# Linear-attention block with gated MLP: denominators, their broadcast and the first gate/up tiles put into other gaps

## The chip, the cores and the metric

The kernel runs on one core of one Trainium2 chip. The metric is the device time of one execution in microseconds (us). The engines of a core are called here as the profile does: PE (TensorE, matmuls), PEld (its weight loads), DVE (VectorE), ACT (ScalarE), POOL (GpSimd) and SP (the queue that issues the transfers).

## What is computed

The input x has 2048 tokens of 640 values. It is normalized once, and the result xn feeds two branches:

```python
xn = layernorm(x)
qkv = xn @ wqkv                                # 32 heads of 20
phi = lambda t: where(t > 0, t + 1, exp(t)) + 1e-6
pq, pk = phi(q), phi(k)
kv  = einsum("bhsd,bhse->bhde", pk, v)         # one 20x20 matrix for each head
z   = pk.sum(over s)
num = einsum("bhqd,bhde->bhqe", pq, kv)
den = einsum("bhqd,bhd->bhq", pq, z) + 1e-6
s   = (num / den) @ wo
g   = silu(((xn @ w_gate) * (xn @ w_up)) @ w_down)   # inner width 1728
out = x + s * g
```

All matrices are bf16. The attention is linear: keys and values are first summed up to `kv` and `z`, and then applied to the queries.

## The kernel before

The five engines have a program each and are tied together by counting semaphores only; the order of the work on each engine is written out by hand. Tokens are cut into 16 tiles of 128 rows, four of which make a chunk of 512 columns (`NCH` = 4 chunks `c`). The model width of 640 is cut into five tiles of 128 (`KD`, indices `k`, `m`, `i`), the inner width of 1728 into 14 (`NF`, index `f`), the last of which has 64 rows. The on-chip accumulator PS has eight banks of 512 fp32 columns.

The stages follow one another like this:

1. *Set-up* (L251 to L266, L635). POOL writes constants and index tables, then sets to zero three areas: `Emat` (L264), `KVm` (L265) and `recd` (L266). DVE makes the identity matrix (L636) from an index table and sets to one the columns of `v_tm` that yield the sum z (L720).
2. *Normalization and transposes.* DVE takes the statistics of the tiles in order (L662 to L665); ACT takes those of chunk 2 (L536, L537). DVE applies them (L688); PE transposes (L315), DVE copies the result to `xnT` (L698).
3. *Queries, keys, values.* PE forms a query tile (L343) or a key or value tile (L360 for 512 columns, L361 for 128), ACT takes exponentials (L553, L560) or copies values (L563), DVE finishes phi (L707 and L709, L716 and L718). Within the second chunk DVE also makes a mask of the heads, `Emat` (row h has ones in the 20 columns of head h) and `ET` in `emit_setup2` (L638 to L656).
4. *Key-value products* (L396 to L405): five accumulations over 16 tiles. ACT takes out the column z (L588), DVE masks the product into `KVm` (L762) and forms `Zm` (L768).
5. *Denominators* (L408 to L411): for each chunk five matmuls give 32 heads x 512 tokens, on partitions 0 to 31 of banks 4 to 7. DVE adds the epsilon (L771), takes the reciprocal (L773), and converts it into the chunk's columns of `recd` (L775).
6. *Numerators* `ot` (L413 to L422): 20 tiles of 128 features x 512 tokens, two or three matmuls each, in banks 0 and 1 by turns; ACT copies them to `oT` (L593).
7. *Broadcast and projection* (L424 to L458). `emit_rbc` spreads the reciprocals of a chunk over the features with one matmul for each feature tile, `Emat` as the weights and `recd` as the moving operand (L433), in banks 4 and 5; DVE multiplies `oT` by the result (L782). `emit_s` multiplies by `Wo` (L450 for 512 columns, L451 for 128), ACT copies the result to `s_tm` (L599). The order is rbc 0, rbc 1, s 0, rbc 2, s 1, rbc 3, s 2, s 3.
8. *Gate and up, down* (L465 to L510): for each of the 4 x 14 tiles five gate matmuls (L478) and five up matmuls (L484); gate tiles use banks 0 and 1 by turns, up tiles banks 2 and 3. ACT copies gate (L608), DVE multiplies it by up into `hT` (L794). Down (L502, L503), sigmoid (L617) and the final products (L806 to L813) of a chunk follow when gate and up of the next chunk have been issued.

The transfers are issued by SP: x, `Wqkv` after the first twelve tiles of x, `Wo`; `Wu` when the last value tile is done, `Wg` and the down weights when the last key-value product is done, as they take the places of arrays no longer in use.

The waits around the change: an `ot` tile waits until ACT has copied the tile two before it (L418); an rbc matmul waits for the reciprocals of its chunk (L429) and for DVE's product two before it (L431); a projection chunk waits for all five products of its chunk (L442); the first gate tile waits for ACT's last copy of the projection (L473).

Of the kernel before, what the change touches and what calls it, by code (L numbers as in the profile page):

```python
# [6 lines left out]
ALU = mybir.AluOpType  # L7
# [5 lines left out]
def bass_recurrent_scan__linear_attn_block__glu_gated_bilinear__prompt_kernel(  # L13
# [40 lines left out]
    with es:  # L54
# [62 lines left out]
        R9a = es.enter_context(nc.sbuf_tensor("R9a", [P, S], bf16))  # L117
        R9b = es.enter_context(nc.sbuf_tensor("R9b", [P, 2 * CW], f32))
        recd = R9a[:, :]
        dtmp = R9b[0:H, 0:CW]  # L120
        rtmp = R9b[0:H, CW:2 * CW]
# [41 lines left out]
        s_pool2 = sem("s_pool2")  # L163
# [21 lines left out]
        s_rec = sem("s_rec")  # L185
        s_ot = sem("s_ot")
# [63 lines left out]

        block = es.enter_context(nc.Block())  # L251

        @block.gpsimd
        def _(eng):
            nc.gpsimd.memset(consts[:, 0:1], EPS_LN)
            nc.gpsimd.memset(consts[:, 1:2], EPS_DEN)
            nc.gpsimd.memset(consts[:, 2:4], 0.0)
            nc.gpsimd.memset(zcol[:, :], 0.0)
            nc.gpsimd.iota(tI160[:, :], pattern=[[P, KD], [-DH, H]], base=0, channel_multiplier=1)
            nc.gpsimd.iota(ti128[:, :], pattern=[[1, P]], base=0, channel_multiplier=-1).then_inc(s_pself, 1)  # L260
            eng.wait_ge(s_pself, 1)
            nc.gpsimd.tensor_copy(ti128f[:, :], ti128[:, :])
            nc.gpsimd.tensor_copy(tI160f[:, :], tI160[:, :]).then_inc(s_pool, 1)
            nc.gpsimd.memset(Emat, 0.0)  # L264
            nc.gpsimd.memset(KVm_flat, 0.0)  # L265
            nc.gpsimd.memset(recd, 0.0).then_inc(s_pool2, 1)  # L266
# [31 lines left out]
        def _(eng):  # L298
# [96 lines left out]
            eng.wait_ge(s_vact, NT)  # L395
            for i in range(KD):  # L396
                hmin, nh = headband(i)
                col0 = (DH + 1) * hmin
                N = (DH + 1) * nh
                bb = i % 2  # L400
                if i >= 2:
                    eng.wait_ge(s_kvbdve, i - 1)
                for t in range(NT):
                    ins = mm(PS[:, 512 * bb:512 * bb + N], pk_tm[:, t, P * i:P * i + P], v_tm[:, t, col0:col0 + N], start=(t == 0), stop=(t == NT - 1))  # L404
                ins.then_inc(s_kvb, 1)  # L405

            eng.wait_ge(s_kvbdve, KD)
            for c in range(NCH):  # L408
                for k in range(KD):
                    ins = mm(PS[0:H, 512 * (4 + c):512 * (4 + c) + CW], Zm[:, k, :], pqT[:, k, CW * c:CW * c + CW], start=(k == 0), stop=(k == KD - 1))  # L410
                ins.then_inc(s_den, 1)  # L411

            for c in range(NCH):  # L413
                for m in range(KD):
                    j = KD * c + m
                    ks = band(m)
                    if j >= 2:
                        eng.wait_ge(s_otact, j - 1)  # L418
                    ob = j % 2
                    for ii, k in enumerate(ks):  # L420
                        ins = mm(bank(ob), KVm[:, k, P * m:P * m + P], pqT[:, k, CW * c:CW * c + CW], start=(ii == 0), stop=(ii == len(ks) - 1))
                    ins.then_inc(s_ot, 1)  # L422

            def emit_rbc(c):  # L424
                for m in range(KD):
                    j = KD * c + m
                    if j == 0:
                        eng.wait_ge(s_erdy2, 1)
                    eng.wait_ge(s_rec, max(c + 1, 1 + (j % 2)))  # L429
                    if j >= 2:  # L430
                        eng.wait_ge(s_onorm, j - 1)  # L431
                    rb = 4 + (j % 2)
                    mm(bank(rb), Emat[:, P * m:P * m + P], recd[:, CW * c:CW * c + CW], start=True, stop=True).then_inc(s_rbc, 1)  # L433
# [4 lines left out]
            def emit_s(c):  # L438
                for tt in range(TPC):
                    t = TPC * c + tt  # L440
                    if tt == 0:
                        eng.wait_ge(s_onorm, KD * (c + 1))  # L442
                        if c == 0:
                            eng.wait_ge(dma_wo, 16)
                            eng.wait_ge(s_rec, NCH)
# [8 lines left out]
            emit_rbc(0)  # L454
            for c in range(NCH):
                if c + 1 < NCH:
                    emit_rbc(c + 1)
                emit_s(c)  # L458
# [5 lines left out]

            def emit_gu(c):  # L465
                for f in range(NF):
                    m = NF * c + f
                    rows = P if f < NF_FULL else F_REM
                    if m == 0:
                        eng.wait_ge(dma_wg, 16)  # L470
                        eng.wait_ge(dma_wu, 16)
                        eng.wait_ge(s_otact, KD * NCH)
                        eng.wait_ge(s_sact, NT)  # L473
                    if m >= 2:
                        eng.wait_ge(s_gcp, m - 1)
                    gb = m % 2
                    for k in range(KD):
                        ins = mm(PS[0:rows, 512 * gb:512 * gb + CW], Wg[:, k, P * f:P * f + rows], xnT[:, k, CW * c:CW * c + CW], start=(k == 0), stop=(k == KD - 1))  # L478
                    ins.then_inc(s_gu, 1)
                    if m >= 2:  # L480
                        eng.wait_ge(s_h, m - 1)
                    ub = 2 + m % 2
                    for k in range(KD):
                        ins = mm(PS[0:rows, 512 * ub:512 * ub + CW], Wu[:, k, P * f:P * f + rows], xnT[:, k, CW * c:CW * c + CW], start=(k == 0), stop=(k == KD - 1))  # L484
                    ins.then_inc(s_gu, 1)
# [20 lines left out]
            emit_gu(0)  # L506
# [6 lines left out]
        def _(eng):  # L513
# [57 lines left out]
            pending_sqrt = [c for c in range(2, NCH) if c not in ACT_SUM_CHUNKS]  # L571
# [13 lines left out]
            for i in range(KD):  # L585
                bb = i % 2
                eng.wait_ge(s_kvb, i + 1)
                act(zcol[:, i:i + 1], PS[:, 512 * bb + DH:512 * bb + DH + 1], ACT.Copy).then_inc(s_kvbz, 1)  # L588
            for c in range(NCH):
# [4 lines left out]
            for t in range(NT):  # L594
                if t == 0:
                    eng.wait_ge(s_tr, NTR)
                eng.wait_ge(s_s, t + 1)
                sb = 6 if (t % 2 == 0) else 2
                act(s_tm[:, t, :], slot2(sb, D), ACT.Copy).then_inc(s_sact, 1)  # L599

            def emit_g_act(c):
                for f in range(NF):
                    m = NF * c + f
                    rows = P if f < NF_FULL else F_REM
                    eng.wait_ge(s_gu, 2 * m + 1)
                    if m >= RG:
                        eng.wait_ge(s_h, m - RG + 1)
                    act(g_sb[0:rows, m % RG, :], PS[0:rows, 512 * (m % 2):512 * (m % 2) + CW], ACT.Copy).then_inc(s_gcp, 1)  # L608
# [10 lines left out]
            emit_g_act(0)  # L619
# [6 lines left out]
        def _(eng):  # L626
# [11 lines left out]
            def emit_setup2():  # L638
                eng.wait_ge(s_pool2, 1)
                eng.wait_ge(s_erdy, 1)  # L640
                v.tensor_copy(
# [78 lines left out]
            tok_ones = dmark(v.memset(R4[:, :].rearrange("p (g j) -> p g j", j=DH + 1)[:, :, DH:DH + 1], 1.0))  # L720
# [6 lines left out]
            for c in ACT_SUM_CHUNKS:  # L727
                emit_mvtiny(c)
# [3 lines left out]
            dve_stats3_done = False  # L732
            tok_mask = None
            for c in range(NCH):
                if c + 2 < NCH:
                    emit_Tcp(c + 2)
                if c == 0:
                    for cc in range(3, NCH):
                        if cc not in ACT_SUM_CHUNKS:
                            emit_stats(cc)  # L740
# [3 lines left out]
                for tt in range(TPC):  # L744
                    emit_kdve_tile(TPC * c + tt)
                    if qc is not None:
                        emit_qdve_tile(qc, tt)
                    if c == 0 and tt == 1:
                        for cc in range(3, NCH):
                            emit_apply(cc)  # L750
# [3 lines left out]

            eng.wait_ge(s_dself, tok_mask)
# [13 lines left out]
            for c in range(NCH):  # L769
                eng.wait_ge(s_den, c + 1)  # L770
                tok = dmark(v.tensor_scalar(dtmp, PS[0:H, 512 * (4 + c):512 * (4 + c) + CW], EPS_DEN, None, op0=ALU.add))  # L771
# [3 lines left out]
                v.tensor_copy(recd[0:H, CW * c:CW * c + CW], rtmp).then_inc(s_rec, 1)  # L775
                eng.wait_ge(s_rec, c + 1)
            for c in range(NCH):
# [5 lines left out]
            eng.wait_ge(s_ot, KD * NCH)  # L783

            def emit_h(c):
                hb = hT[c % 2]
                for f in range(NF):
                    m = NF * c + f
                    rows = P if f < NF_FULL else F_REM
                    if f == 0 and c >= 2:  # L790
                        eng.wait_ge(s_y, TPC * (c - 1))
                    eng.wait_ge(s_gcp, m + 1)
                    eng.wait_ge(s_gu, 2 * m + 2)
                    v.tensor_tensor(hb[0:rows, f, :], PS[0:rows, 512 * (2 + m % 2):512 * (2 + m % 2) + CW], g_sb[0:rows, m % RG, :], ALU.mult).then_inc(s_h, 1)  # L794
# [20 lines left out]
            emit_h(0)  # L815
# [32 lines left out]
```

## Time and profile before

| | us |
|---|---|
| median of 4 runs | 355.93 |
| lowest, highest | 354.06, 356.73 |
| span of the profiled execution | 354.9 |

Where the stages lie in the profiled execution, by its timeline:

| stage | from | to |
|---|---|---|
| set-up, statistics, first transposes | 0 | 22.1 |
| queries, keys, values | 22.1 | 101.5 |
| key-value products | 101.6 | 107.8 |
| denominators | 107.8 | 112.3 |
| `ot` tiles | 112.5 | 126.1 |
| broadcasts and projection | 126.1 | 163.3 |
| gate and up, down, end | 163.3 | 354.9 |

A line of the timeline has the start, the length (both us), the engine, the line in the code, the operation, output and input names, the shape, and the number of instructions that were merged; in brackets stands how long the engine had been idle before, and who released it. Busy lengths of PE are modelled and overlap, since matmuls are pipelined: the distance between the starts of two matmuls tells what one takes of PE's time, the length doesn't. R is the name of most work areas of the kernel, PS that of the accumulator, R9a that of `recd`, R9b that of the denominators' work area.

### The profile page before, as it was taken

The page shows a single profiled execution, that of the slowest core. Times are in us where ns is not written, and L with a number is a line of the kernel's source. Part 1 is how long each engine was busy: PE and PEld are TensorE (multiplying, and loading weights), DVE is VectorE, ACT ScalarE, POOL GpSimd, SP SyncE. Part 2 cuts the span into 40 slices and gives each one's busy share as a digit, 9 for nine tenths or more (in the row PEclk, how much of TensorE's full clock was granted, in tenths as well). Part 3 has the DMA queues.
Part 4 walks back from the last instruction along what each step waited for, and adds up shares of the span by engine and source line. Part 5 has one row for each costly group of instructions (what it writes and reads, how often), then busy time and mean ns, then how long its engine had stood idle before and what let it go on. Part 6 is the DMA issues. An engine that isn't in the chain of part 4 may idle for free.

```text
span 354.9 us, 4525 instructions
## 1 busy us (share of the span) xinstructions
PE 315.5 (89%) x1806; PEld 154.6 (44%) x1840; DVE 186.7 (53%) x312; ACT 116.8 (33%) x192; POOL 6.4 (2%) x15
## 2 busy tenths in 40 slices
PE   0277898999988969898999999999999999999993
PEld 0232444555573214454444444554444544445451
DVE  7876979666547992411333333365332563335555
ACT  1182373555532823333222222213221222221120
POOL 7000000000000000000000000000000000000000
PEclk9999999999999987999999999999999999999998
DMA  7930000000059600005300000011000110000111
GB/s 217 340 109 0 2 0 3 0 2 0 3 178 359 212 0 0 2 0 186 112 0 2 1 0 3 0 39 37 0 2 0 37 39 0 0 2 18 39 55 38
DMA packets 11124, 18.06 MB, mean 51 GB/s; under 512 B 672, under 2 KB 9184, under 8 KB 11104
## 3 DMA queue, kind: packets, MB, share of 16 engines
q1 hardware_dynamic: 11104, 17.78, 14.5%
q8 instruction: 14, 0.23, 0.3%
q14 instruction: 6, 0.05, 0.0%
HBM read 15.16 MB, written 2.62 MB: 50 GB/s over the span
## 4 chain that ended last, share of the span: by engine, by line
PE 77%; DVE 15%; ACT 4%; issue 2%; POOL 0%; POOLq 0%; DVEq 0%; ACTq 0%
PE PS L478 17%; PE PS L484 17%; PE PS L502 14%; PE PS L360 8%; PE PS L343 5%; PE PS L450 5%; PE PS L503 4%; DVE R9b L773 4%; PE PS L361 2%; DVE R L782 2%; PE PS L404 2%; PE PS L451 1%; DVE R L636 1%; DVE statsb L663 1%; DVE statsb L662 1%
## 5 line engine op out<-in xcount | busy, mean ns | idle before, releaser
L794 DVE TENSOR_TENSOR R<-PS,R 128x512 bf16<-128x512 f32 (+1 forms) x56 | 38.6, 690 | 90.1 <-PE PS L484 90.1
L478 PE MATMUL PS<-xnT,R 128*128 128x512 bf16 (+1 forms) x277 | 69.1, 380 | 0.9 <-ACT R L599 0.9
L484 PE MATMUL PS<-xnT,R 128*128 128x512 bf16 (+1 forms) x271 | 69.1, 379 | 0.6
L502 PE MATMUL PS<-R 128*128 128x512 bf16 (+1 forms) x216 | 62.8, 380 | 0.0
L608 ACT ACTIVATE R<-PS 128x512 bf16<-128x512 f32 (+1 forms) x56 | 33.4, 597 | 85.7 <-PE PS L478 81.0
L503 PE MATMUL PS<-R 128*128 128x128 bf16 x224 | 49.0, 219 | 0.5 <-issue 0.2
L360 PE MATMUL PS<-R,xnT 128*128 128x512 bf16 x155 | 44.2, 379 | 1.5 <-DVE R L718 1.5
L478 PEld LDWEIGHTS PS<-xnT,R 128*128 128x128 bf16 (+1 forms) x280 | 27.0, 99 | 34.9 <-ACT R L608 2.1
L484 PEld LDWEIGHTS PS<-xnT,R 128*128 128x128 bf16 (+1 forms) x280 | 27.6, 99 | 32.8
L502 PEld LDWEIGHTS PS<-R 128*128 128x128 bf16 x224 | 21.8, 97 | 31.6 <-issue 8.9
L361 PE MATMUL PS<-R,xnT 128*128 128x128 bf16 x160 | 35.0, 219 | 0.3
L806 DVE TENSOR_TENSOR R<-PS,R 128x640 f32<-128x640 f32 x16 | 13.2, 824 | 31.1 <-ACT R L617 31.1
L617 ACT ACTIVATE R<-PS 128x640 f32<-128x640 f32 x16 | 11.3, 703 | 55.2 <-PE PS L503 55.2
L343 PE MATMUL PS<-xnT,R 128*128 128x512 bf16 x96 | 27.1, 425 | 2.5 <-DVE R L709 1.5
L315 PE MATMUL PS<-R 128*128 128x128 bf16 x80 | 7.8, 265 | 19.6 <-DVE R L688 16.8
L360 PEld LDWEIGHTS PS<-R,xnT 128*128 128x128 bf16 x160 | 15.6, 98 | 20.7 <-issue 1.2
L450 PE MATMUL PS<-Wo,R 128*128 128x512 bf16 x78 | 23.7, 405 | 0.0
L503 PEld LDWEIGHTS PS<-R 128*128 128x128 bf16 x224 | 21.9, 98 | 0.0
L599 ACT ACTIVATE R<-PS 128x640 bf16<-128x640 f32 x16 | 11.3, 703 | 25.0 <-PE PS L451 25.0
L782 DVE TENSOR_TENSOR R<-PS,R 128x512 bf16<-128x512 f32 x20 | 12.8, 686 | 12.3 <-PE PS L433 12.3
L451 PE MATMUL PS<-Wo,R 128*128 128x128 bf16 x80 | 18.2, 227 | 0.1
L343 PEld LDWEIGHTS PS<-xnT,R 128*128 128x128 bf16 x100 | 9.9, 106 | 15.9 <-issue 4.4
(72 smaller groups left out, 283.3 us busy)
## 6 DMA issues: line engine op xcount, KB each, us to landing
R<-in_A_x_dram SPq DMA_DIRECT2D x16, 160.0 KB, 3.7
R<-in_A_x_dram SPq DMA_DIRECT2D x4, 640.0 KB, 7.7
out_dram<-stage SPq DMA_DIRECT2D x16, 160.0 KB, 1.8
R<-in_A_wqkv_dram SPq DMA_DIRECT2D x1, 2400.0 KB, 11.8
R<-in_B_w_up_dram SPq DMA_DIRECT2D x1, 2160.0 KB, 8.0
R<-in_B_w_gate_dram SPq DMA_DIRECT2D x1, 2160.0 KB, 9.2
R<-in_B_w_down_dram SPq DMA_DIRECT2D x1, 2080.0 KB, 14.7
Wo<-in_A_wo_dram SPq DMA_DIRECT2D x1, 800.0 KB, 11.6
```

Of the source, the lines that this page charges most:

```text
L343: ins = mm(bank(qb), Wqkv[:, k, P * m:P * m + P], xnT[:, k, CW * c:CW * c + CW], start=(k == 0), stop=(k == KD - 1))
L360: mm(PS[:, 512 * kb:512 * kb + 512], xnT[:, k, P * t:P * t + P], Wqkv[:, k, wcol:wcol + 512], start=(k == 0), stop=(k == KD - 1))
L361: ins = mm(PS[:, 512 * (kb + 1):512 * (kb + 1) + D - 512], xnT[:, k, P * t:P * t + P], Wqkv[:, k, wcol + 512:wcol + D], start=(k == 0), st ...
L450: mm(PS[:, 512 * sb:512 * sb + 512], oT[:, k, P * t:P * t + P], Wo[:, k, 0:512], start=(k == 0), stop=(k == KD - 1))
L451: ins = mm(PS[:, 512 * (sb + 1):512 * (sb + 1) + D - 512], oT[:, k, P * t:P * t + P], Wo[:, k, 512:D], start=(k == 0), stop=(k == KD - 1))
L478: ins = mm(PS[0:rows, 512 * gb:512 * gb + CW], Wg[:, k, P * f:P * f + rows], xnT[:, k, CW * c:CW * c + CW], start=(k == 0), stop=(k == KD ...
L484: ins = mm(PS[0:rows, 512 * ub:512 * ub + CW], Wu[:, k, P * f:P * f + rows], xnT[:, k, CW * c:CW * c + CW], start=(k == 0), stop=(k == KD ...
L502: mm(PS[:, 512 * yb:512 * yb + 512], hb[0:rows, f, P * tt:P * tt + P], w_d(f, rows, 0, 512), start=(f == 0), stop=(f == NF - 1))
L503: ins = mm(PS[:, 512 * (yb + 1):512 * (yb + 1) + D - 512], hb[0:rows, f, P * tt:P * tt + P], w_d(f, rows, 512, D), start=(f == 0), stop=(f ...
L608: act(g_sb[0:rows, m % RG, :], PS[0:rows, 512 * (m % 2):512 * (m % 2) + CW], ACT.Copy).then_inc(s_gcp, 1)
L782: v.tensor_tensor(oT[:, m, CW * c:CW * c + CW], bank(4 + (j % 2)), oT[:, m, CW * c:CW * c + CW], ALU.mult).then_inc(s_onorm, 1)
L794: v.tensor_tensor(hb[0:rows, f, :], PS[0:rows, 512 * (2 + m % 2):512 * (2 + m % 2) + CW], g_sb[0:rows, m % RG, :], ALU.mult).then_inc(s_h, 1)
```

## The change

It moves and reshapes the work between the key-value products and the gate/up stage, so that the engines have it in other forms and at other places:

- *POOL's three large memsets go.* `recd` is now written in full; the parts of `KVm` that are read but not written by the mask are set to zero by DVE (eight memsets of 112 to 124 columns) after its last key tile; the ones of `v_tm` are set by DVE in four parts in the third and fourth chunk.
- *Denominators on 128 partitions.* The four 128-token tiles of a chunk go to partitions 0 to 31, 32 to 63, 64 to 95 and 96 to 127 (`tile_position`): 80 matmuls of 128 columns instead of 20 of 512. DVE's three operations then have 128x128 for 32x512.
- *They are spread* in groups of eight behind the `ot` tiles 2 to 11.
- *The broadcast* needs, for each of the four groups, weights with zeros outside the group's 32 rows: `Erep4`, made by PE from `Emat` with a selection matrix `Sel4` (two matmuls for each group, behind the first four key-value products) and copied by ACT. A broadcast tile is four matmuls of 128 columns instead of one of 512.
- *Order.* The broadcasts of chunk 0 stand between the `ot` tiles of chunk 3. Behind each broadcast of the chunks 1 to 3 stand two matmuls of a gate/up tile of chunk 0; a fourth gate/up tile stands ahead of the last projection chunk. ACT and DVE take the copies and products of these four tiles in between.
- *Banks.* So that they can run beside the projection, all gate tiles of chunk 0 use bank 0, all its up tiles bank 1; from chunk 1 on it is banks 0 and 1, 2 and 3 as before. The wait for ACT's last projection copy moves to the first gate/up tile of chunk 1.

```diff
-            nc.gpsimd.memset(Emat, 0.0)
-            nc.gpsimd.memset(KVm_flat, 0.0)
-            nc.gpsimd.memset(recd, 0.0).then_inc(s_pool2, 1)
...
+            def emit_erep(g):
+                eb = [2, 4, 6, 2][g]
...
+                mm(PS[:, 512 * eb:512 * eb + 512], Sel4[0:H, g, :], Emat[0:H, 0:512], start=True, stop=True)
+                mm(PS[:, 512 * (eb + 1):512 * (eb + 1) + D - 512], Sel4[0:H, g, :], Emat[0:H, 512:D], start=True, stop=True).then_inc(s_erepmm, 1)
...
-                for k in range(KD):
-                    ins = mm(PS[0:H, 512 * (4 + c):512 * (4 + c) + CW], Zm[:, k, :], pqT[:, k, CW * c:CW * c + CW], start=(k == 0), stop=(k == KD - 1))
-                ins.then_inc(s_den, 1)
+            den_items = [(c, k, g) for c in range(NCH) for k in range(KD) for g in range(TG)]
+            def emit_den(n):
...
+                        ins = mm(PS[H * g:H * g + H, 512 * (4 + c):512 * (4 + c) + P], Zm[:, k, :], pqT[:, k, CW * c + P * g:CW * c + P * g + P], start=(k == 0), stop=(k == KD - 1), tile_position=(0, H * g))
...
                     ins.then_inc(s_ot, 1)
+                    if j >= 2:
+                        emit_den(8)
...
-                    mm(bank(rb), Emat[:, P * m:P * m + P], recd[:, CW * c:CW * c + CW], start=True, stop=True).then_inc(s_rbc, 1)
+                    for g in range(TG):
+                        ins = mm(PS[:, 512 * rb + P * g:512 * rb + P * g + P], Erep4[:, g, P * m:P * m + P], recd[:, c, :], start=True, stop=True)
+                    ins.then_inc(s_rbc, 1)
+                    if filler is not None:
+                        for _ in range(2):
+                            if filler:
+                                filler.pop(0)()
...
-            emit_rbc(0)
+            emit_ot(NCH - 1, lambda m: emit_rbc(0, None, [m]))
             for c in range(NCH):
+                filler = []
+                if c < EARLY_F:
+                    for step in range(2 * KD):
+                        filler.append((lambda cc=c, st=step: emit_gu_step(0, cc, st)))
                 if c + 1 < NCH:
-                    emit_rbc(c + 1)
+                    emit_rbc(c + 1, filler)
+                while filler:
+                    filler.pop(0)()
                 emit_s(c)
...
+                toks = dmark(v.memset(Sel4[0:H, :, :], 0.0))
+                eng.wait_ge(s_dself, toks)
+                for g in range(TG):
+                    dmark(v.tensor_copy(Sel4[0:H, g, H * g:H * g + H], ident128[0:H, 0:H]))
...
-            tok_ones = dmark(v.memset(R4[:, :].rearrange("p (g j) -> p g j", j=DH + 1)[:, :, DH:DH + 1], 1.0))
+                    if (c == NCH - 2 and tt == 0) or (c == NCH - 1 and tt >= 1):
...
+                        dmark(v.memset(R4[:, :].rearrange("p (g j) -> p g j", j=DH + 1)[:, nh4 * cc:nh4 * cc + nh4, DH:DH + 1], 1.0))
...
+                if b0 > lo:
+                    dmark(v.memset(KVm[:, i, lo:b0], 0.0))
+                if hi > b1:
+                    tok_mask = dmark(v.memset(KVm[:, i, b1:hi], 0.0))
```

## The prediction, made before the result was known

> **What bounds the kernel now.** I read the page first, then the chain of waits, the timeline from 0 to 34 us and from 106 to 170 us, and last the busy times by stretch. The page says that TensorE is the engine to follow:
>
> ```profile
> PE 315.5 (89%) x1806; PEld 154.6 (44%) x1840; DVE 186.7 (53%) x312; ACT 116.8 (33%) x192; POOL 6.4 (2%) x15
> PE   0277898999988969898999999999999999999993
> PEclk9999999999999987999999999999999999999998
> ```
>
> From the 19th slice on (163 us, gate, up and down) PE is full: 175.6 of 176.7 us. Nothing is to be won there unless matmuls are moved out of it. The loss lies before: in the first three slices, and in the 15th and 16th (124 to 142 us), where PE thins out and the clock drops. The stretches between the end of the key-value products and gate/up (columns: stretch, its length, then busy us and instructions of PE, weight load, DVE, ACT, POOL, then the clock):
>
> ```profile
> 112.23:126.11 13.88, 13.04 (x51) 3.62 (x53) 13.57 (x10) 10.91 (x19) 0.00 (x0) 1.00 0.62 225
> 126.11:133.03 6.92, 4.24 (x12) 1.00 (x10) 6.51 (x11) 0.80 (x2) 0.00 (x0) 0.81 0.00 0
> 133.03:140.47 7.44, 7.39 (x40) 3.78 (x40) 0.93 (x2) 2.11 (x3) 0.00 (x0) 0.72 0.00 0
> 140.47:143.50 3.03, 1.87 (x8) 0.67 (x8) 2.56 (x5) 0.70 (x1) 0.00 (x0) 1.00 0.00 0
> ```
>
> From 126.11 PE waits for DVE, and the first block of the output projection (133.03 on) runs at a reduced clock. The timeline shows what DVE did:
>
> ```profile
> 123.43 3.34 DVE L773 RECIPROCAL R9b<-R9b 32x512 f32<-32x512 f32 x1
> 126.81 0.41 DVE L775 CAST R9a<-R9b 32x512 bf16<-32x512 f32 x1
> 128.09 0.38 PE L433 MATMUL PS<-R9a,R 128*128 128x512 bf16 x1 [1.38 <-DVE R L782]
> 128.69 0.38 PE L433 MATMUL PS<-R9a,R 128*128 128x512 bf16 x1 [0.22 <-DVE R L782]
> ```
>
> Four reciprocals of 3.34 us run on 32 of 128 lanes; the scaling of `oT` (L782, 0.69 us) starts only after the last, and then sets a pace of about 0.63 us for broadcast matmuls that need 0.216 us. At the start, DVE and not the loads is late:
>
> ```profile
> 2.06 5.07 DVE L636 TENSOR_SCALAR R<-ti128f 128x128 bf16<-128x128 f32 x1 [2.06 <-POOL tI160f L263]
> 4.19 2.94 DVE L662 BATCH_NORM_STATS2 statsb<-R 128x6 f32<-128x320 bf16 x1
> 5.24 1.80 POOL L266 MEMSET R9a<- 128x2048 bf16 x1
> 7.21 0.21 DVE L665 BATCH_NORM_AGGREGATE mv<-statsb 128x2 f32<-128x12 f32 x1
> ```
>
> L636 takes 5.07 us, though a similar operation (L645, 128x160) takes 0.22. It ends at 7.13, just behind POOL's last memset (7.04), and the statistics started at 4.19 end with it.
>
> **What the Trainium skill says.** "SBUF — State Buffer", section "SBUF: two separate sides": VectorE and GpSimd share a port pair, held for a whole instruction, and the loser is blocked. The 5.07 us agree. "TensorEngine Tiling (Array Packing)", section "Key Properties": a change of the tiling mode drains TensorE. The trace has one such change without another wait:
>
> ```profile
> 110.85 1.46 PE L410 MATMUL PS<-R 128*32 128x512 bf16 x6
> 112.23 0.76 PEld L421 LDWEIGHTS PS<-R 128*128 128x128 bf16 x5 [0.42 <-issue]
> 112.46 1.46 PE L421 MATMUL PS<-R 128*128 128x512 bf16 x5 [0.16 <-issue]
> ```
>
> The twenty L410 start 0.216 us apart from 107.81, so the last starts at 111.92 and the next should at 112.14; it starts at 112.46. The change cost 0.32 us. "TensorE: Matmul & The Clock Gate", section "What's actually happening": the clock halves after a mostly idle window of about 3.4 us. It agrees: between 133.03 and 137.2 a pair of projection matmuls (512 and 128 columns) takes 0.53 us, later 0.27.
>
> **The change part by part.**
>
> *Start.* The POOL memsets go. L636 then takes about 0.22 us and the first tile's statistics run from 4.19: 0.36 + 0.40 + the hand-over give an aggregate at 5.05 for 7.21. That is -2.1 us (-1.5 to -2.9). The later tiles, 3.7 us after issues 0.45 us apart, are there in time; the next limit, the landing of `Wqkv` at 6.4 + 11.8 = 18.2, stays ahead of the first query matmul (22.12, then 20.0).
>
> *Memsets on DVE.* The key mask stage gets a memset of 32x512 (0.48 us by L720's row) and four 32x32 copies (about 0.1 each): 0.9 us. DVE has no gap from 53.75 to 64.4, and PE's L360 at 62.28 starts right after L718 (61.40 + 0.82), so all of it is on the path: +0.9 (0.7 to 1.1). The ones for `v_tm` (four memsets of 128) lie in gaps of DVE before L716 (0.3 to 1.4 us). The zeros of `KVm`, 944 elements in eight memsets, 0.9 us plus their starts, fit in DVE's 1.62 us of idle before L762. Both at nothing.
>
> *Erep4.* Four pairs of 512 and 128 columns, 4 x 0.27 = 1.1 us, between the key-value products (no other wait there), with two mode changes each, since Sel4 has 32 rows. Exits cost 0.32; entries aren't shown, between 0 and 0.32. I take 0.25 for any change: entries a bit cheaper. 8 x 0.25 = 2.0. Sum +3.1 (1.1 to 3.7). The four ACT copies (0.70 each, by L599) fit beside the 1.07 us of the next product.
>
> *Denominators among the `ot` tiles, 107.81 to 129.56 (end of the first broadcast chunk), 21.75 us now.* The 20 matmuls of 512 columns become 80 of 128 into four column groups: 80 x 0.056 = 4.5 us. They are put as groups of 8 behind ten `ot` tiles: 20 mode changes, 20 x 0.25 = 5.0 us. New sum: two tiles without (5 matmuls, 1.1), ten tiles (26 x 0.216 = 5.6) + 4.5 + 5.0, three tiles at ACT's pace (3 x 0.65 = 1.95), the last chunk with its five broadcasts (13 x 0.216 + 20 x 0.056 = 3.9): 22.1 us, +0.3. ACT's 0.65 a tile no longer counts, as a tile takes PE 1.5 us. DVE's chain shrinks to a quarter in columns: 3.34/4 for the reciprocal, about 1.4 us in all for 4.5; the fourth is over while the next three tiles run, so no wait remains.
>
> *First projection block, 129.56 to 140.47, 10.9 us.* Broadcast of the second chunk 20 x 0.056 = 1.1 (the ten gate/up matmuls beside it, 2.16, are owed anyway) and 20 pairs at full clock, 5.4: 6.6, so -4.35. This needs PE kept warm.
>
> *Broadcasts of chunks 2 and 3.* 2.77 us each now (140.47 to 143.24, 148.62 to 151.39). With two gate/up matmuls behind each, one step takes PE 0.224 + 0.432 = 0.66 us, DVE's pace is 0.63: the wait is filled. 1.1 each, -3.3.
>
> *Projection to gate/up.* PE's wait for ACT's last copy (0.9 us before L478) moves to the second chunk, where it is long over: -0.9.
>
> *One bank each for gate and up in the first chunk.* Up's bank is free when DVE is done: it starts 0.27 after the last up matmul's slot, takes 0.69, PE sees it 0.06 to 0.15 later: 1.02 to 1.11 us against 1.08 of gate matmuls. ACT's (0.20 + 0.60 + 0.15) fits. +0.5 for ten tiles (0 to 1.0).
>
> Sum: -2.1 + 0.9 + 3.1 + 0.3 - 4.35 - 3.3 - 0.9 + 0.5 = -5.85; 355.93 - 5.85 = 350.1 us.
>
> **The rivals.** *Mode changes are free.* For it: weight loads are otherwise drawn ahead everywhere. Against it: the 0.32 us. Then 28 x 0.25 = 7.0 us less: 343.1. *The denominators eat the gain.* All 28 changes cost 0.32 (+2.0), and weight loads of the column groups aren't hidden, so that a small matmul takes 0.1 us (the 97 ns of a weight load in the row of L410; +3.5): 355.6. For it: each of the 80 has its own load, where now 20 loads stand beside 512 columns. Against it: loads stay hidden beside 147 columns in L404. *Slower.* In addition the thinned `ot` stage halves the clock for two windows, as at 130.4 to 137.2 (6.8 us at half clock, +3.4), and the single banks cost their 1.0: 355.6 + 3.4 + 0.5 = 359.5. Against it: PE's array would still be some 60% occupied, where the window that brought it on had four broadcasts, 0.9 us, in 3.4.
>
> **How the numbers follow.** Forecast 0.52, free changes 0.20, gain eaten 0.18, slower 0.10. The range runs from next to the free case, 343.5, to beyond the third, 356.0, and leaves the slower case out. Faster by over 1% (under 352.4) takes in the second case and most of the first, where the change cost may run somewhat higher: 0.66; within 1%: 0.24; slower: 0.10.
>
> **What would show it.** L636's successor near 0.2 us and the first query matmul near 20.0; gaps of 0.2 to 0.3 us around each group of eight denominators; no half clock after the `ot` stage; no PE wait for the broadcasts; 3.3 us from the first broadcast of chunk 2 to the next projection; gate/up tiles of the first chunk 2.16 to 2.25 us apart. A group of eight should lengthen its tile by 0.45 + 0.5 = 0.95 us: the forecast is wrong if that is over 1.2 or under 0.7, or if the reduced clock is still there.

## The result, and the profile after

The changed kernel takes 341.43 us (median of 10 executions; 341.28 to 342.53) against 355.45 us (median of 16, with the first four; 353.17 to 356.73). The ratio is 0.961, with a 95% interval of 0.958 to 0.963: 14.0 us less, where 5.8 us were forecast. The direction was right; the time lies below the range, and even below the rival with free mode changes (343.1). Executions of the changed kernel lie in two groups about 1 us apart (341.3 to 341.5, and 342.5), and the profiled ones of each differ in how soon PE reaches its full pace in the query stage; the one shown below, 341.45 us, has it early, the profiled one of before has it late.

The page of the changed kernel first:

```profile
PE 307.8 (91%) x1931; PEld 155.7 (46%) x1968; DVE 172.9 (51%) x328; ACT 119.8 (35%) x196; POOL 1.4 (0%) x12
PE   0477888999988999999999999999999999999993
PEclk9999999999999999999999999999999999999998
```

PE has no thin slice left in the middle, and the reduced clock there is gone.

The busy times by stretch, cut where the stages begin and end; columns: stretch, its length, then busy us and instructions of PE, weight load, DVE, ACT, POOL, then the clock. After:

```profile
18.86:97.95 79.09, 70.44 (x451) 36.57 (x461) 58.33 (x131) 40.11 (x62) 0.00 (x0) 1.00 0.02 7
97.95:106.33 8.38, 7.41 (x89) 5.76 (x91) 2.68 (x17) 3.67 (x9) 0.00 (x0) 1.00 0.74 264
106.33:122.50 16.17, 15.64 (x149) 6.24 (x150) 8.42 (x16) 11.37 (x20) 0.00 (x0) 1.00 0.78 275
122.50:126.25 3.75, 3.48 (x32) 2.10 (x31) 3.67 (x7) 1.17 (x2) 0.00 (x0) 1.00 0.02 4
126.25:131.69 5.44, 5.39 (x40) 3.07 (x40) 1.07 (x2) 2.11 (x3) 0.00 (x0) 1.00 0.00 0
131.69:134.97 3.28, 3.28 (x32) 2.05 (x31) 2.85 (x5) 1.30 (x2) 0.00 (x0) 1.00 0.00 0
156.70:339.60 182.90, 176.01 (x950) 83.52 (x968) 75.31 (x100) 44.25 (x70) 0.00 (x0) 0.99 0.09 29
```

Before, the stretches that answer to them are:

```profile
22.12:101.58 79.46, 72.30 (x451) 37.07 (x461) 57.04 (x119) 40.11 (x62) 0.00 (x0) 1.00 0.00 1
101.58:107.81 6.23, 5.49 (x80) 5.30 (x80) 2.25 (x10) 0.85 (x5) 0.00 (x0) 1.00 0.95 344
107.81:129.56 21.75, 19.03 (x75) 5.87 (x77) 20.05 (x16) 11.71 (x20) 0.00 (x0) 1.00 0.59 207
171.95:354.90 182.95, 176.26 (x950) 83.70 (x967) 75.98 (x101) 43.55 (x69) 0.00 (x0) 0.99 0.04 15
```

The last row of each block starts with the fifth gate tile, up to which both kernels have done the same work. From there they take the same time; the whole difference, 171.95 - 156.70 = 15.25 us in these two executions, lies ahead of it. That is a little more than the medians show, because the two differ in PE's pace in the query stage. The changed kernel has a second profiled execution (342.48 us, `after_again` below) with the late pace, in which the fifth gate tile starts at 157.73: with the same pace on both sides the difference is 171.95 - 157.73 = 14.2 us.

One more thing has to be known for the table. In the profiled execution of the changed kernel the first `ot` matmul has no record: its weight load is there at 106.10, and the matmul started at about 106.11, not at the 106.33 at which the stretches above are cut (how this is seen is told below). The table uses 106.11.

By stage, with 2.16 us of gate/up work taken out of each stretch that holds a moved tile:

| stage | forecast | measured in the traces |
|---|---|---|
| start to first query matmul | -2.1 | 18.86 - 22.12 = -3.3 |
| queries, keys, values (memsets on DVE) | +0.9 | 79.09 - 79.46 = -0.4; with the same pace 80.17 - 79.46 = +0.7 |
| key-value products, Erep4 | +3.1 | 8.16 - 6.23 = +1.9 |
| `ot`, denominators, first broadcasts | +0.3 | 16.39 - 21.75 = -5.4 |
| second broadcasts, first projection (129.56 to 140.47 before) | -4.35 | 3.75 + 5.44 - 2.16 - 10.91 = -3.9 |
| broadcasts of chunks 2 and 3 | -3.3 | 2 x (3.28 - 2.16 - 2.77) = -3.3 |
| projection to gate/up | -0.9 | the rest, -1.0 |
| single banks in chunk 0 | +0.5 | 182.90 - 182.95 = 0.0 |

So one row is far off: the stage with the denominators, by 5.7 us. Its timeline (PE alone) shows two groups of eight:

```profile
108.22 0.29 PE L439 MATMUL PS<-R 128*32 128x128 bf16 x8
108.45 0.82 PE L453 MATMUL PS<-R 128*128 128x512 bf16 x3
109.20 0.29 PE L439 MATMUL PS<-R 128*32 128x128 bf16 x8
109.43 0.39 PE L453 MATMUL PS<-R 128*128 128x512 bf16 x1
```

Three `ot` matmuls from 108.45 need 3 x 0.216 = 0.65 us, so the slot of the last ends at 109.10. The group starts at 109.20, and the next `ot` matmul at 109.43. A group of eight lengthens its tile by 0.33 us; the forecast had 0.95.

### The profile page after: what moved, and what is told of

Its sections match the earlier page's. It is cut to its first block, busy times and chain, and to the rows that moved or that the text cites. A ratio compares the mean times of both kernels' runs of the same rounds, so it can differ in the third digit from the quotient of the medians.

```text
span 339.6 us, 4796 instructions
## 1 busy us (share of the span) xinstructions
PE 307.8 (91%) x1931; PEld 155.7 (46%) x1968; DVE 172.9 (51%) x328; ACT 119.8 (35%) x196; POOL 1.4 (0%) x12
## 4 chain that ended last, share of the span: by engine, by line
PE 82%; DVE 10%; ACT 4%; issue 2%; DMA 1%; ACTq 0%; DVEq 0%
PE PS L525 18%; PE PS L531 18%; PE PS L577 15%; PE PS L373 7%; PE PS L496 5%; PE PS L356 5%; PE PS L578 4%; PE PS L453 4%; PE PS L374 2%; PE PS L427 2%; DVE statsb L754 1%; PE PS L497 1%; DVE statsb L753 1%; PE PS L473 1%; DVE R L809 1%
## 5 line engine op out<-in xcount | busy, mean ns | idle before, releaser
L531 PEld LDWEIGHTS PS<-xnT,R 128*128 128x128 bf16 (+1 forms) x280 | 27.1, 99 | 31.3 <-DVE R L886 2.1
L525 PEld LDWEIGHTS PS<-xnT,R 128*128 128x128 bf16 (+1 forms) x280 | 26.7, 99 | 32.0 <-ACT R L679 1.7
L705 ACT ACTIVATE R<-PS 128x640 f32<-128x640 f32 x16 | 11.3, 703 | 55.2 <-PE PS L578 55.2
L356 PE MATMUL PS<-xnT,R 128*128 128x512 bf16 x96 | 25.2, 402 | 3.2 <-DVE R L800 2.3
L496 PE MATMUL PS<-Wo,R 128*128 128x512 bf16 x78 | 21.8, 379 | 0.0
L497 PE MATMUL PS<-Wo,R 128*128 128x128 bf16 x80 | 17.5, 219 | 0.1
L635 ACT ACTIVATE R<-PS 128x640 f32<-128x640 f32 x16 | 11.3, 705 | 16.4 <-PE PS L374 16.3
```

What stands on the lines that cost most here:

```text
L356: ins = mm(bank(qb), Wqkv[:, k, P * m:P * m + P], xnT[:, k, CW * c:CW * c + CW], start=(k == 0), stop=(k == KD - 1))
L496: mm(PS[:, 512 * sb:512 * sb + 512], oT[:, k, P * t:P * t + P], Wo[:, k, 0:512], start=(k == 0), stop=(k == KD - 1))
L497: ins = mm(PS[:, 512 * (sb + 1):512 * (sb + 1) + D - 512], oT[:, k, P * t:P * t + P], Wo[:, k, 512:D], start=(k == 0), stop=(k == KD - 1))
```

## The experiments

All start from the changed kernel (341.43 us).

**The POOL memsets put back.**

```diff
             nc.gpsimd.tensor_copy(tI160f[:, :], tI160[:, :]).then_inc(s_pool, 1)
+            nc.gpsimd.memset(Emat, 0.0)
+            nc.gpsimd.memset(KVm_flat, 0.0)
+            nc.gpsimd.memset(padz[:, :], 0.0).then_inc(s_pool2, 1)
...
             def emit_setup2():
+                eng.wait_ge(s_pool2, 1)
```

> The changed kernel with the three POOL memsets put back in front of the normalization (same places and sizes; the 2048 columns of recd go to a spare area). Theory 1, the memsets held DVE back by what the first query matmul moved (22.12 to 18.86 us): first query matmul back near 22.1, time 341.4 + 3.3 = 344.7. Theory 2, the prediction's reading, in which the first x tile is only there at 4.19 us: first query matmul near 21.0, time 341.4 + 2.1 = 343.5. Theory 3, POOL had no part in it: 341.4.

Measured: 344.70 us (344.67 to 344.71), +3.3, with the first query matmul at 22.10. Theory 1 holds to the tenth. The timeline of this kernel, with the three memsets, and then that of the changed one without:

```profile
2.06 5.07 DVE L729 TENSOR_SCALAR R<-ti128f 128x128 bf16<-128x128 f32 x1 [2.06 <-POOL tI160f L281]
3.05 4.08 DVE L759 BATCH_NORM_STATS2 statsb<-R 128x6 f32<-128x320 bf16 x1
5.24 1.80 POOL L284 MEMSET padz<- 128x2048 bf16 x1
```

```profile
2.06 0.23 DVE L724 TENSOR_SCALAR R<-ti128f 128x128 bf16<-128x128 f32 x1 [2.06 <-POOL tI160f L279]
3.04 0.49 DVE L753 BATCH_NORM_STATS2 statsb<-R 128x6 f32<-128x320 bf16 x1 [0.75 <-DMA R<-in_A_x_dram]
3.96 0.21 DVE L756 BATCH_NORM_AGGREGATE mv<-statsb 128x2 f32<-128x12 f32 x1
```

The identity takes 0.23 us, and the statistics wait for the first tile of x, which is there at 3.04. In the profiled execution of before they started at 4.19. With the memsets it doesn't matter which, since POOL lets DVE go at about 7.04 in either case; without them the landing sets the start. That it sets it early is not luck of one execution: in all ten profiled executions without the memsets the first query matmul starts between 18.80 and 18.91. This fits the port pair of the Trainium skill, "SBUF — State Buffer", section "SBUF: two separate sides", which VectorE and GpSimd share and one of them holds while the other waits.

**Five in a row into the same column group.**

```diff
-            den_items = [(c, k, g) for c in range(NCH) for k in range(KD) for g in range(TG)]
+            den_items = [(c, k, g) for c in range(NCH) for g in range(TG) for k in range(KD)]
```

> The 80 denominator matmuls in the order chunk, group, k, so that five in a row go to the same column group. Theory 1, matmuls in different column groups run beside one another: they no longer can, a group of eight takes 8 x 0.056 = 0.45 us for 0.12, time 341.4 + 3 = 344.4. Theory 2, small matmuls issue at 16 ns whatever their column group: no change, 341.4.

Measured: 343.00 us (342.92 to 343.01), +1.6. A group of eight now holds up the next tile for longer:

```profile
109.40 0.46 PE L439 MATMUL PS<-R 128*32 128x128 bf16 x8
109.79 0.39 PE L453 MATMUL PS<-R 128*128 128x512 bf16 x1
```

It is 0.39 us from the first small matmul to the next `ot` matmul, for 0.23: ten groups by 0.16 are the 1.6 us. Matmuls, shapes, loads and mode changes are the same in number; only the neighbours in the order differ. Theory 2 falls. Theory 1 holds in its mechanism, not in its size: it expected +3.0 us. Neighbours in one group start 0.056 us apart, but the change of group within the eight still lets two groups run beside one another (four steps of 0.056 are 0.22 us; the first and last start of the eight are 0.46 - 0.22 = 0.24 us apart by the merged row).

**Twice the mode changes.**

```diff
                     for ii, k in enumerate(ks):
...
+                        if j >= 2 and (ii == 0 or ii == len(ks) - 1):
+                            emit_den(4)
-                    if j >= 2:
-                        emit_den(8)
```

> The groups of eight denominators split into four behind the first and four behind the last matmul of each ot tile: twenty pairs of mode changes for ten, the same matmuls. Theory 1, a pair costs about 0.2 us as the trace of the changed kernel has it: 341.4 + 2.0 = 343.4. Theory 2, a pair costs 0.5 as in the prediction: 341.4 + 5 = 346.4. Theory 3, changes are free: 341.4.

Measured: 343.62 us (343.59 to 344.59), +2.2: a pair of changes costs 0.22 us, not 0.5. Theory 1.

**All denominators ahead of `ot`.**

```diff
+            eng.wait_ge(s_erep, TG)
+            emit_den(80)
             for c in range(NCH - 1):
                 emit_ot(c)
```

The calls behind the `ot` tiles then find nothing left to issue.

> All 80 denominators ahead of the first ot tile, in one block: one pair of mode changes. Theory 1, small matmuls at 16 ns and ot tiles then at ACT's pace of 0.65 us: 1.5 + 16 x 0.65 = 11.9 us up to the first broadcast for 12.7 now, 340.6. Theory 2, the prediction's sizes (0.056 each): 4.5 + 0.5 + 10.4 = 15.4 us, 344.1.

Measured: 341.97 us (340.90 to 342.05). Theory 2, with the prediction's sizes, is out. The median alone doesn't tell this kernel from the changed one: in its trace (341.92 us) PE has the late pace in the query stage, with 80.16 us from the first query matmul to the key-value products for 79.09. From the first key-value product to the first broadcast it takes 119.52 - 98.98 = 20.54 us, the changed kernel 119.00 - 97.95 = 21.05: 0.5 us less, where theory 1 expected 0.8. The timeline gives the price of the small matmuls directly:

```profile
107.14 1.30 PE L439 MATMUL PS<-R 128*32 128x128 bf16 x80 [0.74 <-DVE R L869]
108.37 1.04 PE L453 MATMUL PS<-R 128*128 128x512 bf16 x4
119.52 0.39 PE L475 MATMUL PS<-recd,Erep 128*128 128x128 bf16 x4
```

80 matmuls with their weight loads, and the change back, take 108.37 - 107.14 = 1.23 us; the forecast had 4.5 us for the matmuls alone. The records of the single matmuls start in fours: four within 0.01 us, one for each column group, and the next four 0.056 us later. Twenty steps of 0.056 are 1.12 us, 14 ns for a matmul, and 0.1 us is left for the change back. The 16 tiles up to the first broadcast then take (119.52 - 108.37)/16 = 0.70 us each, ACT's pace with two banks. That gives back about three quarters of the 9 x 0.22 = 2.0 us that the nine saved pairs of changes won.

**Fillers behind the broadcasts.**

```diff
-                    emit_rbc(c + 1, filler)
+                    emit_rbc(c + 1)
```

> The gate/up tiles of chunk 0 stand behind the five broadcasts of a chunk instead of between them; nothing else is changed. Theory 1, they fill PE's waits for DVE: the broadcasts of chunks 1 to 3 take 2.8 to 3.1 us each again instead of 1.1 to 1.6 beside the fillers, 341.4 + 4.9 = 346.3, more if the clock halves. Theory 2, the waits came from the late reciprocals alone and the fillers hide nothing: 341.4.

Measured: 346.17 us (346.14 to 346.18), +4.7. Theory 1. Its timeline from the second chunk's first broadcast on, then the changed kernel's from the second on:

```profile
122.84 0.38 PE L473 MATMUL PS<-recd,Erep 128*128 128x128 bf16 x4 [0.22 <-DVE R L899]
123.50 0.38 PE L473 MATMUL PS<-recd,Erep 128*128 128x128 bf16 x4 [0.27 <-DVE R L899]
124.10 0.38 PE L473 MATMUL PS<-recd,Erep 128*128 128x128 bf16 x4 [0.22 <-DVE R L899]
```

```profile
123.64 0.39 PE L473 MATMUL PS<-recd,Erep 128*128 128x128 bf16 x4
124.08 0.38 PE L525 MATMUL PS<-xnT,R 128*128 128x512 bf16 x1
124.30 0.39 PE L473 MATMUL PS<-recd,Erep 128*128 128x128 bf16 x4
124.52 0.38 PE L525 MATMUL PS<-xnT,R 128*128 128x512 bf16 x1
124.74 0.38 PE L531 MATMUL PS<-xnT,R 128*128 128x512 bf16 x1
124.95 0.39 PE L473 MATMUL PS<-recd,Erep 128*128 128x128 bf16 x4
```

The broadcasts follow at nearly the same distance, 0.60 to 0.66 us, set by DVE's products; with the fillers PE has work in between and no wait in brackets. (One filler's record is missing: from 123.64 to 124.08 it is 0.44 us, a broadcast of 0.22 and a matmul of 0.22.)

**The long reciprocal chain back.**

```diff
+                for _ in range(3):
+                    tok = dmark(v.reciprocal(rtmp, dtmp))
+                    eng.wait_ge(s_dself, tok)
                 tok = dmark(v.reciprocal(rtmp, dtmp))
```

> Each of the four reciprocals is computed four times (the same operands, the result unchanged): DVE's chain for a chunk is about as long as before the change, 4.4 us. Theory 1, the short chain is what lets DVE start scaling early: the first product of oT moves from 119.5 to about 128 us, PE waits for it and the half clock returns: 341.4 + 8.4 = 349.8, with one to two windows at half clock 351.5 to 353. Theory 2, the gain lies in PE's own work and the chain's length doesn't count: 341.4.

Measured: 351.48 us (351.36 to 351.58), +10.05. Theory 1, with its half clock. The timeline, and the busy times by stretch:

```profile
128.48 1.29 DVE L902 TENSOR_TENSOR R<-PS,R 128x512 bf16<-128x512 f32 x2
129.32 0.58 PE L473 MATMUL PS<-recd,Erep 128*128 128x128 bf16 x4 [7.90 <-DVE R L902]
```

```profile
119.50:125.90 6.40, 1.90 (x14) 0.95 (x14) 6.12 (x9) 1.57 (x3) 0.00 (x0) 1.00 0.01 4
125.90:132.73 6.83, 3.41 (x18) 2.04 (x19) 5.12 (x8) 0.83 (x2) 0.00 (x0) 0.50 0.00 0
```

PE waits 7.90 us for DVE in one piece, and the clock granted from 125.9 to 132.7 is 0.50. Taking back the short chain on 128 lanes (0.95 us for a reciprocal, 3.34 before) costs more than any other of these edits. These costs are no shares of the gain: the memsets, the fillers and the chain together cost 3.3 + 4.7 + 10.05 = 18 us, more than the 14.0 us that the change won, since each was taken back in an order of work in which the others stand.

**Sel4 in a gap of DVE.** The memset and the four copies were moved from the second chunk's mask stage to the third chunk, behind its second key tile.

```diff
             def emit_setup2():
-                toks = dmark(v.memset(Sel4[0:H, :, :], 0.0))
...
                 for tt in range(TPC):
+                    if c == NCH - 2 and tt == 2:
+                        emit_sel()
```

> Sel4's memset and copies moved from the key mask stage in the second chunk to the third chunk, where DVE waits for ACT. Theory 1, they are on the path where they stand now (PE waits 0.65 us for DVE there, 0.1 before the change): 341.4 - 0.5 = 340.9. Theory 2, the wait is made up later in the stage: 341.4.

Measured: 340.78 us (340.75 to 341.68), -0.65. Theory 1: this addition was on the path, as forecast. The stage of queries, keys and values shrinks by as much, from 79.09 to 78.40 us, both with the early pace. It costs what DVE's rows have for it (the changed kernel, mask stage):

```profile
53.52 0.27 DVE L728 MEMSET Sel<- 32x256 uint32 x1
53.83 0.39 DVE L731 COPY Sel<-R 32x32 bf16<-32x32 bf16 x4
58.66 0.39 PE L373 MATMUL PS<-R,xnT 128*128 128x512 bf16 x1 [0.65 <-DVE R L809]
```

**One block behind the second `ot` tile.**

```diff
-                    if j >= 2:
-                        emit_den(8)
+                    if j == 1:
+                        eng.wait_ge(s_erep, TG)
+                        emit_den(80)
```

> All 80 denominators in one block behind the second ot tile, so that ACT has two tiles to copy meanwhile. Theory 1, nine pairs of mode changes of 0.22 us go and ACT's pace of 0.65 us a tile takes over only in part: 11.2 us up to the first broadcast for 12.7 now, 340.0. Theory 2, ACT's pace takes it all back: 341.2.

Measured: 340.80 us (340.68 to 341.75), -0.6 against the changed kernel: between the two theories. From the first key-value product to the first broadcast it takes 118.28 - 97.94 = 20.34 us for 21.05, 0.7 less. ACT copies two tiles while the block runs, but its pace takes back nearly two thirds of the 2.0 us that the nine saved pairs won.

**The three together**, with the fourth Erep4 pair behind the fifth key-value product, and the changed kernel beside it on the same chip.

```diff
-                if i < TG:
+                if i < TG - 1:
                     emit_erep(i)
+                if i == KD - 1:
+                    emit_erep(TG - 1)
```

> The changed kernel once more, beside the next one on the same chip: 341.4.

> Three edits together: the block of 80 denominators behind the second ot tile, Sel4 made in the third chunk, and the fourth Erep4 pair behind the fifth key-value product, where PE waits 1.0 us for DVE. If the three add up: 341.4 - 0.6 - 0.6 - 0.4 = 339.8; if the moved pair delays ACT's column z or its first ot copies: 340.2.

Measured: 341.99 us (341.47 to 342.48) for the changed kernel, 339.58 us (339.53 to 339.75) for the three together; against the kernel before 0.956, with an interval of 0.953 to 0.959. This version beats both kernels. Its trace has PE's early pace in the query stage. Set against the changed kernel's trace with the early pace it gains 1.9 us, where the three estimates sum to 1.6. The stages show the parts: queries, keys, values 78.41 for 79.09 (-0.7, Sel4), key-value products up to the first `ot` matmul 7.67 for 8.16 (-0.5, the moved pair, which has no run of its own), from there to the first broadcast 12.19 for 12.89 (-0.7, the block).

## Why the prediction was wrong

*The step that failed* is "80 x 0.056 = 4.5 us" with "20 x 0.25 = 5.0 us" in the stage of the denominators. Both terms were too large, for one reason each: 1.1 us was measured for the first and 2.2 us for the second.

The 0.056 us is what 128 columns cost when matmuls follow one another through the whole array. Here neighbours in the order go to different column groups and run beside one another: four of them take the 0.056 us that the forecast had for one. The 80 took 1.12 us, and put into an order in which five neighbours share a group they cost 1.6 us more. The Trainium skill, "TensorE: Matmul & The Clock Gate", section "Part 3: Packing small matmuls — row/col tiling", says that tiles of the array work concurrently and gives 2.38 times the speed for three column tiles; the runs agree in kind, with 14 ns for a matmul in four column groups where a stream through the whole array needs 56. The prediction drew on the price of a mode change alone and left this out.

The 0.25 us for a mode change was read from a single gap of 0.32 us. A pair costs 0.22 us, by the doubling experiment, so about 0.11 us for one change. The rest of the 0.32 us was no time at all, but a matmul without a record. The same can be seen in the changed kernel, where no change of mode stands ahead of the first `ot` matmul, beside the kernel without fillers, whose code is the same up to there:

```profile
106.10 0.76 PEld L453 LDWEIGHTS PS<-R 128*128 128x128 bf16 x5 [0.93 <-DVE R L867]
106.33 0.81 PE L453 MATMUL PS<-R 128*128 128x512 bf16 x3 [0.97 <-DVE R L867]
106.74 0.60 ACT L672 ACTIVATE R<-PS 128x512 bf16<-128x512 f32 x1 [1.18 <-PE PS L453]
```

```profile
106.06 0.76 PEld L453 LDWEIGHTS PS<-R 128*128 128x128 bf16 x5 [0.94 <-DVE R L867]
106.07 1.25 PE L453 MATMUL PS<-R 128*128 128x512 bf16 x5 [0.75 <-DVE R L867]
106.71 0.60 ACT L672 ACTIVATE R<-PS 128x512 bf16<-128x512 f32 x1 [1.18 <-PE PS L453]
```

In the second the matmul starts 0.01 us behind its load, as in each of the ten other profiled executions of the changed kernel and its variants, and ACT copies the first tile, of two matmuls, about 0.65 us behind the load. In the first the copy comes just as early, though the first recorded matmul starts 0.22 us later, which is the time of one matmul. So it is the second, and the first left no record. The trace has 52 weight loads and 49 matmuls of `ot`; the other two missing ones explain the gaps at 112.16 and 116.63 in the same way. Before the change there are 52 loads and 50 matmuls, and ACT's first copy at 112.88 comes 0.65 us behind the load at 112.23. The `ot` matmul there thus started at about 112.25 and not at 112.46: leaving the column groups cost 112.25 - 112.14 = 0.1 us.

Ten pairs at 0.22 are 2.2 us for 5.0, and 80 matmuls 1.1 for 4.5: together 6.2 us less. The stage's miss is 5.7, as two smaller terms went the other way: the third tile waits for ACT's first copy (107.19 to 107.48, 0.3 us), and the last eight tiles (116.40 to 122.50, 6.1 us) took 0.25 us more than forecast.

*Start* (-2.1, measured -3.3). The mechanism is confirmed by putting the memsets back. The size was off because the first tile's start at 4.19 us in one execution was taken for a fixed time; in the changed kernel it was 3.04. The stated bounds, -1.5 to -2.9, came from that same execution.

*Memsets on DVE* (+0.9). Right that they are on the path; the cost was 0.65 us, by moving them. The memset was the smaller item: it runs as 256 words of 32 bits in 0.27 us, not 512 elements in 0.48. In the table the stage became shorter nevertheless (-0.4), because PE's pace at its beginning differs: the first ten query matmuls run at half pace in both traces, the next ten took 4.16 us before (from 27.66) and 2.33 us after (from 24.40). Beside the second profiled execution of the changed kernel, in which these ten took 3.86 us, the stage is 80.17 - 79.46 = 0.7 us longer, which agrees with the cost by moving.

*Erep4* (+3.1, measured +1.9). Products and pairs took what was forecast, the two changes around each pair about 0.2 us instead of 0.5 (the last matmul of the first product starts at 98.91 and takes 0.064, so its slot ends at 98.98; to 99.45 it is 0.47 us, less 0.27 for the pair). Four times 0.3 us is the whole miss of 1.2.

*First projection* (-4.35, measured -3.9). At full clock throughout (1.00 in the stretch from 126.25), as forecast: its 40 matmuls took 5.44 us. The missing 0.4 us lies in the first of the second chunk's broadcasts, which waited for DVE (it starts at 122.88, and PE was free at 122.50). "TensorE: Matmul & The Clock Gate", section "What's actually happening", which the prediction cites for a mostly idle window, speaks of an idle one; the four broadcasts from 128.09 on, ahead of the half clock before the change, are 4 x 0.216 = 0.86 us of matmuls, so in this trace the window was mostly and not wholly idle.

*Broadcasts of chunks 2 and 3, projection to gate/up* (-3.3 and -0.9): measured -3.3 and -1.0. *Single banks* (+0.5): nothing; ACT and DVE stay within the 1.08 us.

*The rivals.* "Mode changes are free" came nearest in time and is half right: they aren't free, but the 28 changes cost about 2.2 + 4 x 0.2 = 3.0 us, 4.0 less than forecast. That it lies near the result is in part luck, as it left the matmuls at 4.5 us. "The denominators eat the gain" assumed the loads of the column groups in the open; a matmul with its load took 14 ns. "Slower" needed a half clock in the thinned `ot` stage, and none came there. By its own last sentence (a group over 1.2 us or under 0.7) the forecast was wrong: 0.33.

## What to carry to other kernels

Narrow outputs put side by side into the column groups of the array cost about a quarter each if neighbours in the order go to different groups (here 14 ns for 56); order the loops so that they do. A single gap in a trace isn't a price: look for the same gap where the suspected cause is absent, and count the matmuls against their weight loads, since a missing record looks like a gap. And when a short DVE chain ahead of PE is spread over all lanes, count the half clock that follows PE's wait along with the wait.

## What the runs showed of the hardware that wasn't expected

- 80 matmuls of 128 columns into four column groups, with a weight load each, took 1.12 us, 14 ns each (1.23 us with the change back to the full array): four start within 0.01 us, the next four 0.056 us later. Five in a row into one group made groups of eight 0.16 us longer.
- A pair of changes between a full array and column groups costs 0.22 us (+2.2 us for ten more); a pair between the full array and 32 rows about 0.2 us (98.98 to 99.45, less 0.27).
- Three POOL memsets in a row (1.97 to 7.04 us) held one DVE operation of 0.23 us for 5.07 us; it was not let in between them.
- Two executions of the changed kernel, the same program, differ in how soon PE reaches its full pace: the second ten query matmuls took 2.33 us in the one of 341.45 us (first row) and 3.86 us in the one of 342.48 us (second row). The whole stage of queries, keys and values took 79.09 us in the first and 80.17 us in the second, and the stages behind it agree within 0.03 us when the cut at the first `ot` matmul is put at 106.11.

```profile
24.40 2.33 PE L356 MATMUL PS<-xnT,R 128*128 128x512 bf16 x10 [1.54 <-DVE R L800]
```

```profile
24.35 3.86 PE L356 MATMUL PS<-xnT,R 128*128 128x512 bf16 x10 [1.11 <-DVE R L800]
```
